# A fused S5 + SwiGLU layer: engine streams emitted with and without a block

## The chip, the cores and the metric

The kernel runs on one core of one Trainium2 chip. A core has five engines that run programs of their own: TensorE (PE in the profile; PEld is its weight load), VectorE (DVE), ScalarE (ACT), GpSimd (POOL) and SyncE (SP). SyncE does no arithmetic here; it issues the transfers between the chip's memory and the on-chip buffer. [...] A transfer raises its semaphore by 16 when all of it has landed, in sixteen updates of 1.

The metric is the device time of one execution in microseconds, as the median over several runs.

## The reference

The input x has 2048 rows of 512 in bfloat16. It is normalised per row, and two branches read the result xn: a state space layer (S5) and a gated feed-forward layer of width 1376. The output is the sum of x and both branches.

```
xn = layernorm(x)
dt = exp(log_dt);  Lam_bar = exp(dt * (Lambda_re + 1j*Lambda_im))
Bu = xn @ (((Lam_bar - 1) / Lam)[:, None] * (B_re + 1j*B_im)).T
h_t = Lam_bar * h_{t-1} + Bu_t            # 2048 steps, 512 complex states
A  = 2 * real(h @ (C_re + 1j*C_im).T) + xn * Dskip
Bf = (silu(xn @ w_gate) * (xn @ w_up)) @ w_down
out = x + A + Bf
```

## The kernel before, in words

The 2048 rows are cut into four chunks of 512. For each chunk the kernel normalises the rows, transposes them, and multiplies them by the gate, up and B matrices on TensorE (`ffn_mm` at line 762, `ssm_b_unit` at line 883). ScalarE takes the products out of the accumulation banks, VectorE does the gating, the rotation of the complex state and the scan along the rows (line 923). The results of both branches are multiplied by w_down (line 966, and line 980 for a left-over strip) and by the prepared C matrices (line 983) into one accumulation bank. VectorE adds that bank to the residual (line 988), and SyncE stores the tile (the `dma` helper, line 405). There are 17 stores, `st_out...`: one per tile of 128 rows, and two for the last tile, whose columns are split into 416 and 96.

No engine is programmed directly. Every step is first a task in a graph (`_Graph.add`) with the buffers that it reads and writes. `_schedule` (line 79) gives each engine an order by estimated costs: TensorE and SyncE keep the order in which their tasks were added, and the others are picked by the length of the path behind them. `_plan` (line 185) turns the dependencies into semaphore waits. `_emit` (line 241) writes one engine's stream: the waits of a task with `wait_ge` (line 244), its instruction, and the update of its semaphore. Each transfer has a semaphore of its own; those of the 17 stores have the numbers 128 to 144 in the order of issue.

Where the streams are written is what this case is about. The function opens a block (line 284; the trace files what the block adds under line 283), and at its end five functions, one for each engine, write their streams into it (lines 1050 to 1071). A block gives every engine a piece of program of its own, to which the main program branches and from which it branches to a common end; at that end the block puts a drain on the engines (not on GpSimd, by `no_gpsimd_drain=True`) and a barrier of all five. In the barrier four engines raise a first semaphore (96), GpSimd waits for all four and raises a second one (97), and the four wait for that.

After its own stream GpSimd waits for the 17 stores, in the order in which they were issued (lines 1069 to 1071). It is the one engine that holds the end of the program until the output has landed.

Ahead of the streams the main program has a barrier of its own, with a few memory fills on GpSimd. The trace files it under line 1085, where the program object is made. It belongs to every program and not to the block.

Of the kernel before, what the change touches and what calls it, by code (L numbers as in the profile page):

```python
# [240 lines left out]
def _emit(eng_obj, stream):  # L241
    for t in stream:
        for sem, val in t.waits:
            eng_obj.wait_ge(sem, val)
        inst = t.fn(eng_obj)
        if t.sem is not None and (t.nsig or t.dma):
            inst.then_inc(t.sem, 16 if t.dma else 1)


def bass_parallel_sum__ssm_conv_s5__swiglu_ffn__prompt_kernel(  # L250
# [30 lines left out]
    g = _Graph()  # L281
    es = ExitStack()
    with es:
        block = es.enter_context(nc.Block(no_gpsimd_drain=True))

        def sb(name, shape, dt):
            return es.enter_context(nc.sbuf_tensor(name, shape, dt))

# [755 lines left out]
        streams = _schedule(g.tasks, engs)  # L1044
# [2 lines left out]
        eng_sems = {e: new_sem("sem_" + e) for e in engs if e != "sp"}  # L1047
        _plan(g.tasks, streams, new_sem, eng_sems)

        @block.sync  # L1050
        def _(e):
            _emit(e, streams["sp"])

        @block.tensor
        def _(e):
            _emit(e, streams["pe"])

        @block.scalar
        def _(e):
            _emit(e, streams["act"])  # L1060

        @block.vector
        def _(e):
            _emit(e, streams["dve"])

        @block.gpsimd
        def _(e):
            _emit(e, streams["pool"])
            for t in streams["sp"]:
                if t.out:  # L1070
                    e.wait_ge(t.sem, 16)


# [26 lines left out]
```

## Time and profile before

| | |
|---|---|
| runs of the kernel, median (lowest to highest) | 179.02 us (178.79 to 179.21), 3 runs |
| profiled execution, span from the first to the last instruction | 176.9 us |
| profiled execution, own time with what lies around the span | not given; the median is 2.1 us above the span |
| TensorE's granted clock | 1.000 |
| busy share of TensorE / VectorE / ScalarE / GpSimd | 98% / 92% / 49% / 6% |
| last VectorE addition (line 988), start | 174.7 us |
| 17 stores, from issue to landing, min / median / max | 1.5 / 1.7 / 2.0 us |

The profile is taken from one execution. Its span runs from the first to the last instruction of the program; the runtime's own work ahead of it and behind it is outside the span and inside the measured time. Semaphore instructions, branches and drains are done by an engine's sequencer (marked with a q, as in POOLq) and count as no busy time, so the table's shares do not show them; they are found by the source line that they belong to. A semaphore instruction's record begins when its wait is satisfied and not when the waiting begins. Beside the instructions the trace keeps the time of every semaphore update, the runtime's semaphores among them.

### The profile page before, as it was taken

To read this page: it belongs to the slowest core of one execution; us is meant where nothing else is said; L and a number is where in the kernel's file an instruction comes from. 1 tells how busy PE (TensorE), PEld (TensorE's weight loads), DVE (VectorE), ACT (ScalarE), POOL (GpSimd) and SP (SyncE) were. 2 spreads that over 40 slices of the span, in tenths; PEclk is the share of its full clock that TensorE was granted. 3 is DMA by queue.
4 is the path that set the end of the run, shared out by engine and by line. 5 is a ranking of instruction groups with operands and counts; after the bars stand their busy time and mean duration, and the time that the engine had idled before them with its cause. 6 is when DMAs were issued, how large, how long until landed. Compare 5 with 4: busy or idle time off the path is not lost.

```text
span 176.9 us, 2385 instructions
## 1 busy us (share of the span) xinstructions
PE 173.8 (98%) x916; PEld 82.7 (47%) x916; DVE 162.4 (92%) x282; ACT 87.3 (49%) x116; POOL 11.0 (6%) x22
## 2 busy tenths in 40 slices
PE   8999999999999999999999999999999999999994
PEld 2894444444444444444444444444444444444543
DVE  2975999799999999999999999999999999999953
ACT  4689989979999569230456554000265520000000
POOL 3040500046000000000000000000000000000000
DMA  5892694855685300002100000001100000000131
GB/s 166 273 371 80 135 125 94 263 120 119 119 262 120 58 0 0 0 4 83 37 0 0 0 0 4 0 0 59 59 0 4 0 0 0 0 0 4 59 119 59
DMA packets 22966, 12.37 MB, mean 70 GB/s; under 512 B 15308, under 2 KB 22956, under 8 KB 22956
## 3 DMA queue, kind: packets, MB, share of 16 engines
q1 hardware_dynamic: 22652, 11.77, 25.4%
q10 hardware_dynamic: 304, 0.46, 0.8%
q8 instruction: 7, 0.11, 0.3%
q14 instruction: 3, 0.02, 0.1%
HBM read 6.46 MB, written 2.10 MB: 48 GB/s over the span
## 4 chain that ended last, share of the span: by engine, by line
PE 98%; DVE 0%; issue 0%
PE pb L762 36%; PE pb L966 20%; PE pb L983 16%; PE pb L883 16%; PE pb L806 4%; PE pb L478 3%; PE pb L980 2%; PE pb L845 2%; PE pb L855 1%; PE pb L585 1%; DVE x_sb L988 0%
## 5 line engine op out<-in xcount | busy, mean ns | idle before, releaser
L923 DVE TENSOR_TENSOR_SCAN rot<-sm,car,rot 128x512 bf16<-128x512 f32 x32 | 38.7, 1264 | 0.0
L774 ACT ACTIVATE sg<-pb 128x1024 bf16<-128x1024 f32 x20 | 20.2, 1025 | 32.1 <-PE pb L762 31.4
L966 PE MATMUL pb<-wd,hT 128*128 128x512 bf16 (+2 forms) x170 | 35.4, 367 | 0.0
L983 PE MATMUL pb<-W,hss 128*128 128x512 bf16 (+2 forms) x136 | 30.4, 366 | 0.0
L762 PE MATMUL pb<-xnT,wu 128*128 128x512 bf16 x120 | 27.9, 379 | 0.0
L966 PEld LDWEIGHTS pb<-wd,hT 128*128 128x128 bf16 x170 | 16.0, 97 | 19.0 <-ACT scrC L730 0.4
L832 ACT ACTIVATE uf<-pb 128x1024 bf16<-128x1024 f32 x20 | 20.5, 1027 | 7.4 <-PE pb L762 7.2
L762 PE MATMUL pb<-xnT,wg 128*128 128x512 bf16 x92 | 21.8, 379 | 0.0
L883 PE MATMUL pb<-xnT,BT 128*128 128x512 bf16 x96 | 21.0, 379 | 0.0
L983 PEld LDWEIGHTS pb<-W,hss 128*128 128x128 bf16 x136 | 12.9, 97 | 14.9
L890 ACT ACTIVATE u_sb<-pb 128x1024 bf16<-128x1024 f32 x16 | 16.3, 1019 | 5.3 <-PE pb L883 5.2
L762 PEld LDWEIGHTS pb<-xnT,wu 128*128 128x128 bf16 x120 | 11.7, 98 | 14.2 <-issue 0.2
L883 PEld LDWEIGHTS pb<-xnT,BT 128*128 128x128 bf16 x96 | 9.4, 98 | 11.3
L988 DVE TENSOR_TENSOR x_sb<-pb,x_sb 128x512 bf16<-128x512 f32 (+2 forms) x17 | 10.9, 655 | 3.5 <-PE pb L983 3.2
L762 PEld LDWEIGHTS pb<-xnT,wg 128*128 128x128 bf16 x92 | 9.0, 98 | 10.6
L834 DVE TENSOR_TENSOR hT<-sg,uf 128x1024 bf16<-128x1024 bf16 x20 | 13.4, 679 | 0.5 <-ACT uf L832 0.5
L483 DVE BATCH_NORM_STATS2 st<-x_sb 128x6 f32<-128x512 bf16 x12 | 7.5, 681 | 3.0 <-DMA x_sb<-in_A_x_dram 3.0
L914 DVE TENSOR_TENSOR rot<-u_sb,cosT 128x2048 bf16<-128x2048 bf16 x8 | 9.7, 1217 | 0.0
L914 DVE TENSOR_TENSOR rot<-rot,sin 128x2048 bf16<-128x2048 bf16 x8 | 9.7, 1218 | 0.0
L914 DVE TENSOR_TENSOR rot<-u_sb,sin 128x2048 bf16<-128x2048 bf16 x8 | 9.7, 1215 | 0.0
L914 DVE TENSOR_TENSOR rot<-rot,cosT 128x2048 bf16<-128x2048 bf16 x8 | 9.7, 1211 | 0.0
L914 DVE TENSOR_TENSOR rot<-rot 128x2048 bf16<-128x2048 bf16 x8 | 9.6, 1215 | 0.0
(93 smaller groups left out, 180.3 us busy)
## 6 DMA issues: line engine op xcount, KB each, us to landing
out_dram<-x_sb SPq DMA_DIRECT2D x15, 128.0 KB, 1.7
x_sb<-in_A_x_dram SPq DMA_DIRECT2D x3, 512.0 KB, 4.6
wd<-in_B_w_down_dram SPq DMA_DIRECT2D x1, 1280.0 KB, 6.6
wu<-in_B_w_up_dram SPq DMA_DIRECT2D x1, 768.0 KB, 4.8
wu<-in_B_w_up_dram SPq DMA_DIRECT2D x1, 608.0 KB, 6.9
x_sb<-in_A_x_dram SPq DMA_DIRECT2D x4, 128.0 KB, 3.2
wg<-in_B_w_gate_dram SPq DMA_DIRECT2D x1, 480.0 KB, 5.8
wg<-in_B_w_gate_dram ACTq DMA_DIRECT2D x1, 448.0 KB, 3.9
```

Source lines behind the costliest of these rows:

```text
L483: return g.add("dve", lambda e, a=a: e.bn_stats(out=st[:, a % 8, :], in_=x_sb[:, a, :]), reads=[("x", a)], writes=[("st", a % 8), ("st0", ...
L762: inst = e.matmul(pbank[0:fs, bk, :].rearrange("p (j t) -> p j t", j=4), lhsT=w[:, kt, i * 128:i * 128 + fs], rhs=xnT[c][:, :, kt, :], sta ...
L774: g.add("act", lambda e: e.activation(out=sg[rows, sl, 0:n, :].rearrange("p a t -> p (a t)"), in_=pair_f32(rows, bk, 512 * n), func=AF.Sil ...
L832: g.add("act", lambda e: e.activation(out=uf[rows, ul, 0:n, :].rearrange("p a t -> p (a t)"), in_=pair_f32(rows, bk, 512 * n), func=AF.Ide ...
L834: g.add("dve", lambda e: e.tensor_tensor(out=hT[rows, hb, i0:i0 + n, :], in0=sg[rows, sl, 0:n, :], in1=uf[rows, ul, 0:n, :], op=ALU.mult), ...
L883: inst = e.matmul(pbank[:, bk, :].rearrange("p (j t) -> p j t", j=4), lhsT=BT[:, ri, kt, pt * 128:(pt + 1) * 128], rhs=xnT[c][:, :, kt, :] ...
L890: g.add("act", lambda e: e.activation(out=u_sb[:, us].rearrange("p r t -> p (r t)"), in_=pair_f32(slice(0, 128), b0), func=AF.Identity), r ...
L914: tt = lambda out, a, b, op, r, w, nm: g.add("dve", lambda e: e.tensor_tensor(out=out, in0=a, in1=b, op=op), reads=r, writes=w, name="%s_% ...
L923: g.add("dve", lambda e, A0=A0, A1=A1, k=k, ri=ri, pt=pt: e.tensor_tensor_scan(out=A1[:, k, ri, :], data0=rr[:, pt:pt + 1].to_broadcast([1 ...
L966: inst = e.matmul(pbank[:, bk, 0:nc_], lhsT=hT[0:fs, hb, i, lt * 128:(lt + 1) * 128], rhs=wd[0:fs, i, c0:c0 + nc_], start=(i == 0), stop=F ...
L983: inst = e.matmul(pbank[:, bk, 0:nc_], lhsT=hss[:, hb, pt, ri, lt * 128:(lt + 1) * 128], rhs=W12[:, ri, pt, c0:c0 + nc_], start=False, sto ...
L988: g.add("dve", lambda e, bk=bk, a=a, c0=c0, nc_=nc_: e.tensor_tensor(out=x_sb[:, a, c0:c0 + nc_], in0=pbank[:, bk, 0:nc_], in1=x_sb[:, a, ...
```

## The change

The block is gone. The same five streams are written straight into the main program, one after the other in the text; each engine still has its own sequence of instructions. GpSimd's waits for the 17 stores are written in the opposite order, so that the last store's comes first in the code. Nothing else is changed: tasks, orders, waits within the streams, buffers and transfers are the same.

```
     g = _Graph()
     es = ExitStack()
     with es:
-        block = es.enter_context(nc.Block(no_gpsimd_drain=True))
-
         def sb(name, shape, dt):
...
         _plan(g.tasks, streams, new_sem, eng_sems)
 
-        @block.sync
-        def _(e):
-            _emit(e, streams["sp"])
-
-        @block.tensor
-        def _(e):
-            _emit(e, streams["pe"])
-
-        @block.scalar
-        def _(e):
-            _emit(e, streams["act"])
-
-        @block.vector
-        def _(e):
-            _emit(e, streams["dve"])
-
-        @block.gpsimd
-        def _(e):
-            _emit(e, streams["pool"])
-            for t in streams["sp"]:
-                if t.out:
-                    e.wait_ge(t.sem, 16)
+        _emit(nc.sync, streams["sp"])
+        _emit(nc.tensor, streams["pe"])
+        _emit(nc.scalar, streams["act"])
+        _emit(nc.vector, streams["dve"])
+        _emit(nc.gpsimd, streams["pool"])
+        for t in [t for t in streams["sp"] if t.out][::-1]:
+            nc.gpsimd.wait_ge(t.sem, 16)
```

## The prediction

> **What bounds the kernel now.** I read the head of the page and its chain of work first, then the answers for the two source lines that the change removes, then the timeline of the last microseconds.
>
> ```profile
> span 176.9 us, 2385 instructions
> ## 4 chain that ended last, share of the span: by engine, by line
> PE 98%; DVE 0%; issue 0%
> ```
>
> The reader is to see that TensorE's matmuls fill 98% of the span without a break. The change touches no matmul, no transfer and no order between them: every engine gets the same stream of instructions as before. So what it can move is what lies ahead of the first matmul and behind the last one. The answer for line 283, the opening of the block, shows what the block leaves in the trace (columns: engine, instruction, count, min/median/max ns, first and last start in us):
>
> ```profile
> L283 ACTq EVENT_SEMAPHORE  x2: 17/17/17, 142.9 to 176.8; - x2
> L283 PEldq EVENT_SEMAPHORE  x2: 51/51/51, 174.7 to 176.8; - x2
> L283 DVEq EVENT_SEMAPHORE  x2: 21/21/21, 175.0 to 176.8; - x2
> L283 SPq EVENT_SEMAPHORE  x2: 17/17/17, 175.5 to 176.8; - x2
> L283 POOLq EVENT_SEMAPHORE  x2: 17/17/17, 176.7 to 176.8; - x2
> L283 ACTq DRAIN  x1: 1054/1054/1054, 141.8 to 141.8; - x1
> L283 PEldq DRAIN  x1: 960/960/960, 173.7 to 173.7; - x1
> L283 DVEq DRAIN  x1: 297/297/297, 174.7 to 174.7; - x1
> L283 SPq DRAIN  x1: 128/128/128, 175.3 to 175.3; - x1
> L283 POOLq COMPARE_BRANCH  x1: 41/41/41, 176.5 to 176.5; - x1
> ```
>
> Four drains, ten semaphore instructions and one branch, all at the end. There is no branch at the beginning and none on four of the five engines. The answer for line 1071 (the store waits) and the last rows of the timeline complete the tail:
>
> ```profile
> L1071 POOLq EVENT_SEMAPHORE  x8: 42/43/43, 168.3 to 176.4; - x8
> ```
>
> ```profile
> 171.04 4.25 SPq L405 DMA_DIRECT2D out_dram<-x_sb  x4
> ...
> 174.67 0.26 DVE L988 TENSOR_TENSOR x_sb<-pb,x_sb 128x96 bf16<-128x96 f32 x1 [0.22 <-PE pb L983]
> ```
>
> The trace's records carry nanoseconds, so the tail can be followed step by step: the last VectorE add starts at 174.673 and takes 0.258; SyncE issues the last store from 174.958 to 175.290; its sixteenth and last semaphore update comes at 176.419. GpSimd's last pair of store waits then runs at 176.442 (43 ns), its branch at 176.529 (41 ns), its two barrier instructions at 176.699 and 176.779 (17 ns each, so GpSimd ends at 176.796), and the other four engines take the release at 176.820 to 176.833, the last of them ending at 176.884. That is the span.
>
> **The time around the span.** The profiled execution has no time of its own in what is shown; its span is 176.88 and the median of the runs is 179.02, so 2.14 us lie outside, and I subtract from 179.02. What lies behind the span is in the trace's record of semaphore updates: the runtime's semaphore 2 is updated nine times between 177.120 and 177.650, the user semaphores are reset from 177.56 to 178.21, and semaphore 2 is updated nine times again from 178.438 to 178.795. The second series has steps of 34, 38, 45, 23, 98, 39, 34 and 46 ns. The first has 34, **210**, 44, 23, 99, 40, 34 and 46. So in the first the third participant came 172 ns late. I infer that it is GpSimd: in the same nine updates ahead of the span the participants' releases, taken backwards, fit TensorE, ScalarE, GpSimd, VectorE, SyncE as the order (SyncE's first record comes first at 0.000, TensorE's last at 0.316). GpSimd thus needs 177.364 - 176.796 = 0.57 us from its last record to its turn, and everything behind waits for it.
>
> **The change part by part.**
>
> 1. Closing barrier and GpSimd's branch, removed. Counted at the span, 176.884 - (176.442 + 0.043) = 0.40 us go. Counted where the time continues, GpSimd's own end moves from 176.796 to 176.485: 0.31 us. I take 0.31, because GpSimd's turn is the late one of the hand-over and the other four reach theirs earlier still. Bounds: 0.31 to 0.40 by these two rows; if GpSimd's 0.57 us shrinks to TensorE's 0.236 (176.884 to 177.120), 0.31 + 0.33 = 0.64.
> 2. The last wait alone. If it holds one semaphore instead of two it is nearer the one-semaphore row of GpSimd (17 ns, line 244) than the pair's 43 ns: another 0.03 us; bounds 0 to 0.03.
> 3. Closing drains, removed: SyncE's ends at 175.475, VectorE's at 174.983, TensorE's at 174.683, ScalarE's long before. All end at least 0.97 us ahead of the wait for the last store at 176.442, which covers them: 0. Without that cover SyncE's would cost 0.13. A loss has no place either, since nothing comes behind them on their engines.
> 4. Opening branches. The trace has no record of one. From the opening barrier's release on SyncE (0.711) to its first load (0.791) are 80 ns; between GpSimd's two barrier instructions at 0.591 and 0.669, with no branch between, are 78. SyncE's own satisfied waits follow one another at 59 to 62 ns. So a branch hides at most 20 ns, and I take 0.02 us earlier loads, since VectorE's first statistics wait for that load and the first transposes for them. Bounds: 0.06 (80 less the 17 ns of the instruction before) gained or, as nothing measures the new layout, 0.06 lost.
> 5. Store waits reversed. GpSimd has nothing queued behind them, and nobody in the program waits for GpSimd any more; only the runtime's hand-over does. What matters is how many instructions stand behind the wait for the last store (semaphore 144). The records show that the compiler does not keep the code's order: the code waits for 128, 129, ... 144, and the trace has the pairs 137+136, 138+135, 139+134, 140+133, 141+132, 142+131, 143+130, 144+129 and, on the branch, 128. The first wait of the list is kept for the last instruction, and the rest are paired from the middle outwards. By the same rule the reversed list ends with 144 alone and has 135+136 to 128+143 ahead of it, all long landed by then except 143, which lands at 176.142. I take nothing behind 144: 0.
> 6. SyncE's queue, the transfers, the planner's orders and every wait inside the streams: nothing is moved past anything: 0.
>
> Sum: 0.31 + 0.03 + 0.02 = 0.36 us; 179.02 - 0.36 = **178.66 us**.
>
> The tail's branch costs more than its 41 ns: from 176.529 to the next record are 170 ns, against 87 from the pair to the branch. [...]
>
> **The rivals.**
>
> - *More goes than the barrier*: GpSimd's slow 0.57 us may belong to the taken branch or to the barrier and not to the runtime. For it: TensorE needs 0.236. Against: no record says what fills it. Then 0.36 + 0.33 = 0.69: 178.33.
> - *Slower: the waits stay in the code's order*. With no instruction behind them to be attached to, the compiler may leave the pairs as written, 144+143 first and 128 last. Then eight satisfied waits stand behind the last landing. At the 87 ns from the last pair to the branch, GpSimd ends at 176.442 + 8 x 0.087 + 0.043 = 177.18 instead of 176.796: 0.38 later, 179.40 (179.38 with term 4). At SyncE's 60 ns it is 0.17 later, 179.17 with term 4. It decides from four instructions on: 0.31 / 0.087 = 3.6. Against it: every list in the trace was reordered.
> - *No change*: the hand-over is held by an engine other than GpSimd whose own path does not shorten; or the runs' spread (178.79 to 179.21) swallows it. About 179.0.
> - *The waits fall away*: trailing waits with nothing behind them are dropped as dead. Then the streams end with the last store's issue at 175.290, 1.5 us ahead of 176.796: 177.5. Little speaks for it.
>
> **How the numbers follow.** Forecast 0.62; more goes 0.14; slower 0.14; no change 0.07; waits dropped 0.03. Of this kernel a measurement tells about 0.2%, that is 0.36 us, from no change, and the forecast sits on that line: I give it 0.33 as faster and 0.29 as within. Faster 0.33 + 0.14 + 0.03 = 0.50. Slower 0.12, the rival without its cheap end. Within: 0.29 + 0.07 + 0.02 = 0.38. The range takes in the forecast with the bounds of terms 1, 2 and 4, the rival in which more goes (178.33, less 0.08 for the runs' spread) and no change with 0.1 of spread: 178.25 to 179.10. Outside are the slower rival and the dropped waits, 0.17.
>
> **What would show each step.** No record of the block's line and no branch; GpSimd's last record a wait for semaphore 144 right after the last landing, about 1.15 us after the last store's issue ends; a span of about 176.5. Eight GpSimd waits within 0.7 us behind the last landing would show the slower rival. The step between the second and the third update of semaphore 2 tells whether GpSimd still holds the hand-over. The prediction is wrong where the matmul chain itself gets longer or shorter: TensorE's first transposes should start at 5.0 and its last matmul at 174.43, both within 0.05.

## The result and the profile after

With 22 runs of each kernel the median goes from 178.80 us to **178.44 us**; the ratio is 0.998, with a 95% interval of 0.9972 to 0.9987. The forecast was 0.36 us less, and 0.36 us less is what was measured (the kernel before stands at 178.80 here and not at 179.02, because more of its runs are counted; the predicted 178.66 lies above the measured 178.44 by that difference). The change is small, but clear: the interval does not take in 1. In microseconds it is 0.23 to 0.50 less, so it is chance that forecast and measurement agree to the hundredth.

The head of the page of the changed kernel, and its answer for line 283, where the block's records were:

```profile
span 176.6 us, 2364 instructions
```

```profile
nothing on L283; most used: ['L760', 'L964', 'L981', 'L881', 'L804', 'L244', 'L912', 'L403', 'L978', 'L583', 'L921', 'L843', 'L853', 'L476', 'L942', 'L772', 'L830', 'L832', 'L1068', 'L986', 'L888', 'L631', 'L481', 'L485', 'L1054']
```

The drains, the barrier and the branch are gone. Of the 21 instructions fewer, the block's records are 15; there is one store wait more, and 7 are matmul records that this trace lacks (909 against 916; no matmul was taken out of the code). The answer for line 1054, where the store waits now stand (columns as for line 283 of the kernel before), and the last rows of the timeline:

```profile
L1054 POOLq EVENT_SEMAPHORE  x9: 17/558/1913, 168.0 to 176.4; - x9
```

```profile
174.65 0.81 SPq L403 DMA_DIRECT2D out_dram<-x_sb  x2
174.85 0.26 DVE L986 TENSOR_TENSOR x_sb<-pb,x_sb 128x96 bf16<-128x96 f32 x1 [0.22 <-PE pb L981]
```

The reader is to see two things. The last VectorE addition starts at 174.85, where it was 174.67: in the two profiled executions the work itself ended 0.18 us apart, in the wrong direction, and the span still fell by 0.25. And a semaphore instruction's record is now up to 1.9 us long, where all eight lasted 42 or 43 ns; the last section says why.

Since the chain of matmuls ends at a slightly different time in each execution, I compare the kernels by what lies **behind the last landing**, the sixteenth update of the last store's semaphore. From the end of that store's issue to the landing are 1.13 to 1.14 us in all ten profiles. What follows is read from one profile of each kernel; the stretch that all have in common, from the end of the first series of updates of semaphore 2 to the last update, takes 1.14 to 1.18 us in all ten. The table has the time behind the landing in us. The runtime's hand-over is the first of the two series of nine updates of its semaphore 2 behind the work, in which the engines take turns. The columns give when the last record of the engine that is late in it ends (GpSimd, or the engine that waits for the stores), when that engine takes its turn, and when the last update of the second series comes. In the nine profiled executions whose own time is on record, that last update, counted from the start of the span, lies 0.17 to 0.18 us above the measured time: what comes off this tail comes off the time.

| kernel | engine | its last record | its turn | last update | ratio to before (95%) |
|---|---|---|---|---|---|
| before | GpSimd | 0.377 | 0.945 (third) | 2.376 | |
| changed | GpSimd | 0.029 | 0.563 (third) | 1.992 | 0.998 (0.9972 to 0.9987) |
| no block, waits as issued | GpSimd | 0.068 | 0.600 (third) | 2.031 | 0.9977 (0.9961 to 0.9993) |
| block, waits reversed | GpSimd | 0.297 | 0.864 (third) | 2.295 | 0.9994 (0.9977 to 1.0011) |
| no block, closing barrier | GpSimd | 0.108 | 0.675 (third) | 2.102 | 0.9974 (0.9959 to 0.9988) |
| no block, SyncE waits | SyncE | 0.022 | 0.138 (fifth) | 1.448 | 0.9931 (0.9909 to 0.9953) |
| no block, VectorE waits | VectorE | 0.035 | 0.176 (fourth) | 1.564 | 0.9961 (0.9944 to 0.9977) |
| no block, ScalarE waits | ScalarE | 0.027 | 0.136 (second) | 1.637 | 0.9964 (0.9953 to 0.9975) |
| no block, TensorE waits | TensorE | 0.035 | 0.221 (first) | 1.720 | one run, 177.99 us |
| block, SyncE waits | GpSimd | 0.387 | 0.955 (third) | 2.385 | 1.0005 (0.9994 to 1.0016) |

For the changed kernel the landing is at 176.606, GpSimd's last record ends at 176.635, the third update comes at 177.169 and the last one at 178.598. Each ratio is to runs of the kernel before from the same series: their median is 178.80 us for the changed kernel, 179.13 for the first four experiments below and 179.02 for the others, so medians of different series cannot be compared. No run of the changed kernel was taken in the series of the experiments.

So the change takes 2.376 - 1.992 = 0.384 us off the tail, against 0.36 in the medians.

### The profile page after: what moved, and what is told of

Read it like the earlier page. It is cut to its first block, busy times and chain, and to the rows that moved or that the text cites. A ratio compares the mean times of both kernels' runs of the same rounds, so it can differ in the third digit from the quotient of the medians.

```text
span 176.6 us, 2364 instructions
## 1 busy us (share of the span) xinstructions
PE 173.2 (98%) x909; PEld 82.5 (47%) x916; DVE 162.4 (92%) x282; ACT 87.1 (49%) x116; POOL 11.0 (6%) x22
## 4 chain that ended last, share of the span: by engine, by line
PE 96%; DMA 1%; DVE 1%; issue 0%; ACT 0%
PE pb L760 36%; PE pb L964 19%; PE pb L881 16%; PE pb L981 16%; PE pb L804 4%; PE pb L978 2%; PE pb L843 2%; DMA x_sb<-in_A_x_dram 1%; PE pb L853 1%; PE pb L583 1%; DVE st L529 0%; DVE xn_sb L516 0%; ACT sd L523 0%; DVE x_sb L986 0%; PE pb L476 0%
## 5 line engine op out<-in xcount | busy, mean ns | idle before, releaser
L964 PE MATMUL pb<-wd,hT 128*128 128x512 bf16 (+2 forms) x166 | 34.7, 366 | 0.3 <-issue 0.2
L981 PE MATMUL pb<-W,hss 128*128 128x512 bf16 (+2 forms) x133 | 29.8, 366 | 0.2
```

Source lines behind the costliest of these rows:

```text
L964: inst = e.matmul(pbank[:, bk, 0:nc_], lhsT=hT[0:fs, hb, i, lt * 128:(lt + 1) * 128], rhs=wd[0:fs, i, c0:c0 + nc_], start=(i == 0), stop=F ...
L981: inst = e.matmul(pbank[:, bk, 0:nc_], lhsT=hss[:, hb, pt, ri, lt * 128:(lt + 1) * 128], rhs=W12[:, ri, pt, c0:c0 + nc_], start=False, sto ...
```

## The experiments

My theory: the time follows GpSimd's own path, from the last landing over its last instruction to its turn in the runtime's hand-over. Each nanosecond taken off that path counts, and what the other engines do beside it does not. The rivals: the reversed order of the waits carries the gain; the barrier cost the time by holding the other engines; the streams start earlier without a block.

**Order of the waits alone.** The changed kernel, its waits in the order of issue:

```
-        for t in [t for t in streams["sp"] if t.out][::-1]:
+        for t in [t for t in streams["sp"] if t.out]:
             nc.gpsimd.wait_ge(t.sem, 16)
```

> No block, as in the changed kernel, but GpSimd waits for the stores in the order in which they were issued. Theory (the time follows GpSimd's own path behind the last landing): the last instruction holds the same two waits in the other order, so GpSimd ends 43 + 23 = 66 ns behind the last landing as in the kernel before, where the changed kernel has 29; 0.04 us more than the changed kernel, 0.32 us less than the kernel before, ratio about 0.998. Rival (the reversal carries the gain): the eight other waits stand behind the last landing in one of the two orders, at 60 to 87 ns each, and this kernel loses 0.5 to 0.7 us against the changed one: ratio 1.001 to 1.002.

Line 1054 in this kernel's answer:

```profile
L1054 POOLq EVENT_SEMAPHORE  x9: 17/43/43, 168.2 to 176.9; - x9
```

There are nine instructions as in the changed kernel, the same pairs, each with its two waits exchanged, and the one with the last store's semaphore stands last in both. GpSimd ends 0.068 us behind the landing instead of 0.029: the reversal is worth 0.04 us, by the trace. The ratio, 0.9977 (0.9961 to 0.9993), is that of the changed kernel within its interval. The first rival falls, and with it the slower case of the prediction: in neither order does anything stand behind the last store's wait.

**The waits reversed, with the block.**

```
             _emit(e, streams["pool"])
-            for t in streams["sp"]:
-                if t.out:
-                    e.wait_ge(t.sem, 16)
+            for t in [t for t in streams["sp"] if t.out][::-1]:
+                e.wait_ge(t.sem, 16)
```

> The block of the kernel before, and only the store waits reversed. Theory: the branch now holds the wait for the last store, and the last pair of waits no longer stands between the landing and the branch; that is 87 ns, so 0.09 us less than before, ratio 0.9995, and GpSimd's branch starts about 25 ns behind the landing instead of 110. The step from the second to the third update of the runtime's semaphore 2 falls from 210 to about 120 ns. Rival (the reversal carries the gain): the whole 0.36 us, ratio 0.998.

Its branch, in the answer for line 283:

```profile
L283 POOLq COMPARE_BRANCH  x1: 41/41/41, 177.2 to 177.2; - x1
```

The landing is at 177.202 and the branch starts at 177.226, so the branch does hold the last wait, and the 0.08 us of the pair ahead of it are gone: GpSimd ends at 0.297 instead of 0.377, the last update comes at 2.295 instead of 2.376. The time cannot resolve that: its interval (0.9994, 0.9977 to 1.0011) takes in the theory's 0.9995, no change, and just so the rival's 0.998. The trace decides: the reversal takes 0.08 us off this tail, not 0.36. One point that I expected was wrong: the step from the second to the third update stays at 210 ns. With the barrier TensorE is released by GpSimd, and so both moved by the same 0.08.

**The barrier put back, without branch and drains.**

```
             nc.gpsimd.wait_ge(t.sem, 16)
+        nc.all_engine_barrier(sem_only=True)
```

> The changed kernel with a closing barrier of all five engines put back, on the same two semaphores, but no branch and no drains. Theory (GpSimd's own path): GpSimd ends about 0.13 us behind the last landing (wait 0.03, release 0.08 later, 0.017 long) instead of 0.377 before and 0.029 changed, so 0.25 us less than before, ratio 0.9986, and 0.10 more than the changed kernel. Rival (the barrier holds the other four engines, and that is what cost the time): the whole gain is gone, ratio 1.000. Rival (the opening without a block): the gain stays whole, 0.36 us, ratio 0.998.

The barrier's records in this kernel, line 1055:

```profile
L1055 ACTq EVENT_SEMAPHORE  x2: 17/17/17, 142.1 to 176.9; - x2
L1055 PEldq EVENT_SEMAPHORE  x2: 51/51/51, 174.0 to 176.9; - x2
L1055 DVEq EVENT_SEMAPHORE  x2: 21/21/21, 175.0 to 176.9; - x2
L1055 SPq EVENT_SEMAPHORE  x2: 17/17/17, 175.6 to 176.9; - x2
L1055 POOLq EVENT_SEMAPHORE  x2: 17/130/242, 176.5 to 176.8; - x2
```

All five engines are held until 176.9 again, as in the kernel before, and still 2.376 - 2.102 = 0.27 of the 0.38 us stay: the ratio is 0.9974 (0.9959 to 0.9988). That the barrier cost the time by holding the others is excluded (it asked for 1.000). The interval does not tell my 0.9986 from the 0.998 of an earlier opening; the trace does. From the landing to the last update this kernel is 0.11 us slower than the changed one, as expected (0.10), and the first load of the changed kernel starts at 0.793 us against 0.791 before: the opening gained nothing.

**Another engine waits.** Four kernels put the 17 waits on another engine. One line of the changed kernel differs (here for SyncE):

```
-            nc.gpsimd.wait_ge(t.sem, 16)
+            nc.sync.wait_ge(t.sem, 16)
```

> The changed kernel with the 17 waits on SyncE, which issues the stores, instead of GpSimd. GpSimd is done at 41 us. Theory (GpSimd needs 0.53 us of its own from its last record to its turn in the runtime's hand-over, and SyncE, which I take for the fifth in it, some 0.25 like TensorE): SyncE's turn comes 0.03 + 0.25 = 0.28 us behind the last landing instead of 0.63, so 0.35 us less than the changed kernel, 0.71 less than before: about 178.1, ratio 0.996. Rival (the half microsecond is what any last engine needs): at most the 0.07 us between the third and the fifth turn, ratio 0.9976 at best.

Line 1054 in the kernel in which SyncE waits:

```profile
L1054 SPq EVENT_SEMAPHORE  x9: 17/28/394, 175.7 to 176.5; - x9
```

SyncE ends 0.022 us behind the landing and takes its turn 0.116 later; GpSimd needs 0.534 in the changed kernel. The last update comes at 1.448, 0.93 us earlier than before and 0.54 earlier than in the changed kernel; I had expected 0.71 and 0.35, since I gave SyncE the 0.25 us of TensorE (0.14 of the difference; another 0.05 is the step behind SyncE's turn, 43 ns here and 98 in the changed kernel). The ratio is **0.9931** (0.9909 to 0.9953), 178.05 us against 179.13 before: faster than the kernel before, and its interval is clear of the changed kernel's.

> The changed kernel with the 17 waits on VectorE. Theory (the engines take their turns in the order TensorE, ScalarE, GpSimd, VectorE, SyncE, and only GpSimd needs half a microsecond from its last record to its turn): the long step of the first series of the runtime's semaphore 2 lies ahead of the fourth update, which comes about 0.03 + 0.15 us behind the last landing (VectorE needed 0.15 in the run in which SyncE waited), and the last update about 1.57 us behind the landing, against 1.45 with SyncE, 1.99 changed and 2.38 before: 0.8 us less than before, ratio 0.9955. Rival (the order of turns is another, and SyncE was quick for another reason): the long step lies elsewhere, or the last update stays at 1.9 to 2.0, ratio 0.998.

> The changed kernel with the 17 waits on ScalarE. Theory: the long step lies ahead of the second update, which comes 0.15 to 0.28 us behind the last landing; with the seven steps that follow (0.32) the last update comes 1.62 to 1.75 us behind it: 0.63 to 0.76 us less than before, ratio 0.996. Rival (any engine that ends last needs half a microsecond, SyncE excepted): second update at 0.56, last update at 2.03, ratio 0.998.

> The changed kernel with the 17 waits on TensorE. Theory: no long step inside the series, since the first participant is the late one; the first update 0.03 + 0.24 to 0.32 us behind the last landing, all eight steps short (0.36 in all), the last update 1.78 to 1.86 us behind the landing. Rival (order of turns is another): a long step inside the series.

The same line in the kernels in which VectorE, ScalarE and TensorE wait:

```profile
L1054 DVEq EVENT_SEMAPHORE  x9: 21/50/832, 174.8 to 176.3; - x9
```

```profile
L1054 ACTq EVENT_SEMAPHORE  x9: 17/563/1919, 168.5 to 176.9; - x9
```

```profile
L1054 PEldq EVENT_SEMAPHORE  x9: 51/51/1380, 173.7 to 176.2; - x9
```

The first series of nine updates has its long step ahead of the fourth update when VectorE waits (1710 ns), ahead of the second when ScalarE waits (1750 ns), and nowhere when TensorE waits (34, 39, 44, 23, 98, 38, 34, 47). So the order of turns that the prediction inferred, TensorE, ScalarE, GpSimd, VectorE, SyncE, is now shown by experiment. From the last record to the turn, TensorE needs 0.19 us, ScalarE 0.11, VectorE 0.14, SyncE 0.12, GpSimd 0.53. VectorE's and ScalarE's last updates, 1.564 and 1.637, are as expected; TensorE's, 1.720, lies under the 1.78 to 1.86 that I expected.

Ahead of the span there is a series of nine updates of semaphore 2 as well: in these traces it takes 370 to 372 ns. Behind the work, when TensorE waits, so that no one else is late, the eight steps add up to 357 ns: the same order of size in both places.

**The block kept, SyncE waits.**

```
             _emit(e, streams["sp"])
+            for t in [t for t in streams["sp"] if t.out][::-1]:
+                e.wait_ge(t.sem, 16)
...
             _emit(e, streams["pool"])
-            for t in streams["sp"]:
-                if t.out:
-                    e.wait_ge(t.sem, 16)
```

> The kernel before with its block, and the 17 waits on SyncE instead of GpSimd, reversed. Theory (with the closing barrier GpSimd leaves last whoever waits for the stores): SyncE's branch, drain and barrier instruction follow the landing, then GpSimd's two; GpSimd ends 0.5 us behind the landing instead of 0.38, the last update comes 2.4 to 2.55 us behind it: no gain, ratio 1.000 to 1.001. Rival (which engine waits decides, barrier or not): 0.9 us less as without the block, ratio 0.995.

Three lines of its answer for line 283:

```profile
L283 POOLq EVENT_SEMAPHORE  x2: 17/17/17, 177.1 to 177.1; - x2
...
L283 SPq COMPARE_BRANCH  x1: 33/33/33, 176.8 to 176.8; - x1
L283 SPq DRAIN  x1: 13/13/13, 177.0 to 177.0; - x1
```

The landing is at 176.779. Now SyncE has the branch and a drain behind it, and GpSimd still closes the barrier: it ends 0.387 us behind the landing (I expected 0.5), and its half microsecond follows as before. The ratio is 1.0005 (0.9994 to 1.0016): no gain. The same move of the waits that takes 0.93 us off the tail of the kernel before when the block goes too takes nothing off with the block. So with the barrier GpSimd is the late one in the hand-over when SyncE waits just as when GpSimd does; that it would be so with the other three was not run.

## Why the prediction was right, by its steps

1. *Closing barrier and branch*: 0.31 forecast, 0.309 measured. The kernel without a block and with its waits as issued ends with a pair of waits that names 144 first, as the last pair of the kernel before does, and has nothing behind it; GpSimd's last record ends 0.377 - 0.068 us earlier behind the landing. The right place to count was GpSimd's end and not the span's, whose end was TensorE's: put against the landing, the span's end moved by (176.884 - 176.419) - (176.635 - 176.606) = 0.436 us, which is too much.
2. *The last wait*: 0.03 forecast, 0.068 - 0.029 = 0.039 us measured, but this is luck. The prediction took it from a last instruction with 144 alone. The trace has 128 and 144 in one instruction, with 136 alone at the beginning, and the 0.039 us come from the order in which the two waits are named. Together, terms 1 and 2 are 0.377 - 0.029 = 0.348 us. The kernel with the barrier alone splits this in another way: 0.377 - 0.108 = 0.269 for the branch with the pair of waits ahead of it, and 0.079 for the barrier.
3. *Closing drains*: 0 forecast. Nothing in the runs speaks against it: the rows of term 1 give 0.311 us and 0.309 is measured, which leaves nothing for the drains. But they were taken out together with the branch, and no run took them out alone. Where one does stand behind the landing, on SyncE in the last experiment, it lasts 13 ns, with 63 from its start to the next record, and not the 0.13 us that the prediction gave for a drain without cover.
4. *Opening branches*: 0.02 forecast, nothing measured (first load at 0.791 and 0.793). No run shows an opening branch. A branch to the block and one from it on every engine is not what the trace has: the kernel before has a single branch record, GpSimd's closing one at 176.529. From the opening barrier's release on SyncE to its first load are 80 ns before and 81 in the changed kernel (0.712 to 0.793).
5. *Reversed waits*: nothing behind the last store's wait, as forecast; the 0.04 us that the reversal does bring stand under term 2. In the changed kernel the other wait of the last pair is settled ahead of the landing and no longer behind it.
6. *GpSimd's path to its turn*: 0.57 forecast to stay. It is 0.53 behind a wait and 0.57 behind a barrier's release, in all six kernels in which GpSimd ends last. These 0.03 us were not in the sum; that they fill the place of the 0.02 of term 4, which did not come, is luck.

The sum of what the trace shows is 0.348 + 0.034 = 0.38 us, against 0.36. The rival in which GpSimd's half microsecond goes too is refuted: it stayed, with and without branch and barrier. The first transposes start at 4.96 in the changed kernel's profile, as asked for. Its last matmul starts at 174.60 and not within 0.05 of 174.43 as I asked for; in the profiles of both kinds of kernel it lies anywhere from 174.43 to 175.20, the latest in one with the block, so that bound was set too tight on one execution and says nothing on the change. The 2.14 us that the prediction put outside the span are one execution's span taken from the median of others; in the 54 runs of the kernel before that have both, 1.7 to 1.8 us lie outside. No term of the sum rests on it.

What stays open is what fills GpSimd's half microsecond. It belongs to GpSimd and not to the wait or the barrier, as the experiments with the other engines show, but the trace has no record between its last instruction and its turn.

## What to carry to other kernels

Where the matmuls fill the span (TensorE is busy for 98% of it here), look at what lies behind the last landing, and count it on the engine that is late in the runtime's hand-over, not at the end of the span. The block's closing instructions cost 0.31 us here (0.35 with the order of the waits); worth more was that without its barrier the stores can be waited for by an engine that leaves quickly (SyncE: 0.12 us from its last record to its turn, and the last update at 1.448, the earliest of the five) instead of GpSimd, the slowest to leave here (0.53 us, last update at 1.992).

## What the runs showed that I had not expected

- In these traces the record of a semaphore instruction with two waits begins when the first of them is satisfied, and the second is waited for inside the record. The last pair of the kernel before, which names 144 first, starts at 176.442, 23 ns behind 144's landing; that of the changed kernel, which names the long landed 128 first, runs from 176.383 to 176.635, and 144 lands at 176.606. That a record begins when the wait is satisfied holds for the first wait alone. With the late store named second, GpSimd's records last up to 1913 ns in the changed kernel, and 40823 in the kernel with the block and the waits reversed; with the same store named first they last 43. The idle time between such records cannot be read without looking at the order of the waits.
- Naming the late semaphore second was also quicker by 0.04 us on GpSimd: 29 ns from landing to end against 68.
- The branch with a wait cost the sequencer 170 ns from its start to its next record on GpSimd, in both kernels with the branch on it; on SyncE it was 166 ns.
- GpSimd needed 0.53 us to leave where the other engines needed 0.11 to 0.19.
